# A Fourier mixing layer in front of a GELU MLP: the complex filter product summed on VectorE, narrower tiles in two stages of the transform

## The chip, the cores and the metric

The kernel runs on one core of a Trainium2 chip. The metric is the device time of one execution in microseconds; lower is better. The figure for the kernel before is the median of three runs; one more execution was taken with the hardware profiler, and all rows and timelines are from that one.

## The reference

Two layers in a row, on x of shape (8, 3008, 256). The first multiplies the spectrum of each batch along the sequence with a complex filter; the second is an MLP with the exact GELU.

```python
X = np.fft.rfft(x, axis=1)                       # 8 batches, 3008 points, 256 channels
y = np.fft.irfft(X * (filt_r + 1j * filt_i), n=3008, axis=1)
h = y.reshape(24064, 256) @ w_in                 # 256 -> 2048
out = (0.5 * h * (1 + erf(h / sqrt(2)))) @ w_out # 2048 -> 256
```

## The kernel before

**The transform.** 3008 = 47 x 64 (NA x NB). The transform is done in matmuls in two steps forward and two back. `s1` is the first forward step (over 47 points, four quarters c of each batch), `s2` the second (over 64 points, for 24 values of an index k), `s2_out` the product with the filter, `s3` the first step back (over 64), `s4` the last (over 47). Between `s1` and `s2`, and between `s3` and `s4`, the data go through DRAM (tensors R1 and R2), where the store and the load regroup them: `r1` loads the spectrum tiles `b_sb`, `r2` the tiles `d_sb`. Batch 0 has functions of its own (`c1`, `c1t`, `c2`, `c3`, `c3t`, `c4`) and runs before everything else, some 38 us. It uses the filters `F` as they were loaded; for batches 1 to 7 these are saved to DRAM (`save_filters`, tensor Fd) and loaded again in another order (`load_filters_again`).

**The MLP.** 24064 rows in 47 tiles of 512. `mm1` does the first matrix (line 635) and ScalarE the GELU (line 638). The second matrix is done for each tile but the first with seven products of quarter matrices in place of eight (`mm2_seven`, line 707). This needs sums of quarters of g on VectorE: `sums_1` (line 676), `sums_2` (line 682), `sums_3` (line 689). Its results are combined on VectorE as groups of output matmuls finish (lines 722 to 736): line 722 copies the first group, 724 and 727 add the third, 729 to 733 the fifth, 736 the last two. Two PSUM banks (`ps_o`) take turns: groups 1, 2 to 3, 4 to 5, 6 to 7. A bank is free for its next groups once VectorE has read it. Output rows are stored from GpSimd's queue (line 754).

**The order.** Tile code with a schedule written out by hand: 16 slots for each tile of the MLP, one `mm1` step (two 512-column matmuls and a GELU) and seven output matmuls to a slot. The transform of batch b is put into the slots of the tiles before its own, with `put(slot, function, ...)`, lines 902 to 978. Every engine runs its own instructions in that order, so an instruction that waits holds all behind it on its engine.

**A third of a batch.** Batches 1 to 7 do `s2`, `s2_out` and `s3` in three thirds u = 0, 1, 2; 21 thirds in all. `s2` of a third stands in slot s2[u], the four products in slots s2[u], +2, +4, +6, `s3` and the first half of its evacuation in slot +10 (+9 in two thirds of batch 1), the other half in the next slot. In a third, before:

- `s2` (line 458): 16 matmuls with stationary tiles of 64x64 and 256 moving columns, into four PSUM banks. The 64 stationary columns are real and imaginary part of 32 frequencies, so the two parts come to lie in different partitions.
- `s2_out` (line 470): four VectorE products of 128x1024, each of a bank (read twice over) with the real and the imaginary filter. The two halves of a complex product are left unsummed.
- `s3` (line 484): 16 matmuls of 64x64 and 512 columns. The summing of real and imaginary parts happens inside the contraction over 64 rows with the table `U`, accumulated over two values of t.
- `s3_out`: ScalarE evacuates four banks to `v_sb` (line 329), SP's queue stores them to R2.

PSUM has eight banks: three for `ps_h` (tag "h", also lent to one bank of each stage), two for `ps_o`, and three of tag "f" for the stages of the transform. The tables are built on GpSimd while the first slots run (`table_1_tiles`, `table_2_parities`, `table_u_rows`, `table_u_pick`, `table_4_rows`). The fold (lines 106 and 107) prepares x of the next batch on VectorE; its loads are issued from GpSimd's queue, each behind a `gate` (line 149), a one-element copy that waits for a product.

Of the kernel before, what the change touches and what calls it, by code (L numbers as in the profile page):

```python
# [31 lines left out]
class _Mix:  # L32
    def __init__(self, ctx, tc, x, filt_r, filt_i, w_in, w_out, out):
# [11 lines left out]
        self.pb = pool("pb", 3)  # L45
# [14 lines left out]
        self.U = c.tile([128, 2, 2, HB], BF16, name="U")  # L60
        self.T4a = c.tile([96, HB, 96], BF16, name="T4a")
        self.T4c = c.tile([96, NA, 2], BF16, name="T4c")
        self.F = c.tile([128, 2, K1, 256], BF16, name="F")
        self.w_in_sb = c.tile([128, 2, self.DFF], BF16, name="w_in_sb")
# [53 lines left out]
    def save_filters(self, k0, k):  # L118

        if "Fd" not in self.st:  # L120
            self.st["Fd"] = self.dram.tile([2, 2, 16, 2, K1, 256], BF16, tag="Fd", name="Fd")
        for t in range(2):
            for q in range(2):
                o = self.st["Fd"][:, q, :, t, k0:k0 + k, :].rearrange("a i k c -> i a (k c)")
                if q:
                    o = o[:, ::-1]
                self.nc.sync.dma_start(out=o, in_=self.F[32 * q:32 * q + 32, t, k0:k0 + k, :])

    def load_filters_again(self, eng, k0, k):

        for o in range(0, 128, 32):
            i = self.st["Fd"][o // 64, :, :, :, k0:k0 + k, :].rearrange("q i t k c -> (q i) t k c")
            f = self.F[o:o + 32, :, k0:k0 + k, :]
            if o < 64:
                eng.dma_start(out=f.rearrange("p t k c -> p t (k c)"), in_=i.rearrange("p t k c -> p t (k c)"))
            else:
                for t in range(2):
                    for e in range(2):
                        eng.dma_start(out=f[:, t, e::2], in_=i[:, t, 1 - e::2])
# [11 lines left out]
    def load_next(self, b, p, c, h):  # L151

        self.gate(self.st[b, "p", p][0:1, 0, 0:1])
        self.load_x_pairs(b + 1, c, h)
# [95 lines left out]
    def weights_4(self, g):  # L250


        ts = self.nc.gpsimd.tensor_scalar
        h, q, self.wt, self.wts = (g.tile([128, 1], FP32, name=n) for n in ("h48", "q48", "wt", "wts"))
        ts(out=h, in0=self.p, scalar1=48.0, scalar2=None, op0=ALU.is_ge)
        ts(out=q, in0=h, scalar1=-48.0, scalar2=-1.5, op0=ALU.mult, op1=ALU.add)
        self.nc.gpsimd.tensor_tensor(out=q, in0=self.p, in1=q, op=ALU.add)
        self.nc.gpsimd.tensor_tensor(out=q, in0=q, in1=q, op=ALU.mult)
        ts(out=q, in0=q, scalar1=2.25, scalar2=-1.0, op0=ALU.is_equal, op1=ALU.mult)
        ts(out=self.wt, in0=q, scalar1=2.0, scalar2=None, op0=ALU.add)  # L260
        ts(out=h, in0=h, scalar1=-2.0, scalar2=1.0, op0=ALU.mult, op1=ALU.add)
        self.nc.gpsimd.tensor_tensor(out=self.wts, in0=self.wt, in1=h, op=ALU.mult)
# [73 lines left out]
    def table_1_tiles(self, g):  # L336
# [4 lines left out]
        for r in (0, 64):  # L341
            v.tensor_copy(out=self.T1s[r:r + NA, 0:48], in_=self.T1[0:NA, 0:48])
# [10 lines left out]
    def table_u_rows(self, g):  # L353

        v = self.nc.gpsimd
        self.u0 = g.tile([128, 2, 2, HB], BF16, name="u0")
        v.tensor_copy(out=self.u0[:, 0], in_=self.T3[:, 0, :, 0:HB])
        v.tensor_copy(out=self.u0[:, 1], in_=self.T3i[:, 0, :, 0:HB])

    def table_u_pick(self, g):  # L360
        to = self.cols
        self.nc.gpsimd.iota(to, pattern=[[0, 2], [64, 2], [33, 2], [2, 16]], base=0, channel_multiplier=0,
                            allow_small_or_imprecise_dtypes=True)
        self.pick = g.tile([128, 128], BF16, name="pick")
        self.nc.gpsimd.tensor_scalar(out=self.pick, in0=to, scalar1=self.p, scalar2=None, op0=ALU.is_equal)

    def table_u(self):
        ps = self.bank("ps_u", "f")
        self.nc.tensor.matmul(ps[:, 0:128], lhsT=self.pick, rhs=self.u0.rearrange("p t r w -> p (t r w)"),
                              start=True, stop=True)  # L370
        self._evac(self.U.rearrange("p t r w -> p (t r w)"), ps[:, 0:128], "act")

    def table_4_rows(self, g):
# [3 lines left out]
        self.T1g = g.tile([NA, 2, 2, 12, 2, 2], BF16, name="T1g")  # L377
        self.T2g = g.tile([128, 2, 12, 2, 2], BF16, name="T2g")
        for x in range(2):
            for r in range(2):  # L380
                t = self.T1[0:NA, 24 * (x ^ r):24 * (x ^ r) + 24].rearrange("p (a k) -> p a k", k=2)
                for j in range(2):
                    v.tensor_copy(out=self.T1g[:, x, r, :, j], in_=t[:, :, ::-1] if j else t)
        t = self.T2.rearrange("p (a k) r j -> p r a j k", k=2)[:, 0, :, 0:2, :]
        for r in range(2):
            for j in range(2):
                v.tensor_copy(out=self.T2g[:, r, :, j], in_=t[:, :, j, ::-1] if j else t[:, :, j])

    def table_4_factors(self, g):
        ps = self.bank("ps_t4", "f")  # L390
        mm = lambda o, n, t, k: self.nc.tensor.matmul(ps[0:96, o:o + n], lhsT=t, rhs=self.eye[0:k, 0:k], start=True, stop=True)
        for x in range(2):
            mm(NA * x, NA, self.T1g[:, x].rearrange("p r a j k -> p (r a j k)"), NA)
        mm(128, 128, self.T2g.rearrange("p r a j k -> p (r a j k)"), 128)
# [46 lines left out]
    def r1(self, b, c):  # L441
        bt = self.pb.tile([128, 6, 256], BF16, tag="b", name="b_sb")
        self.st[b, "b", c] = bt
        v = self.st[b, "R1"].rearrange("n (r k) c -> (n r) k c", r=2)
        self.nc.sync.dma_start(out=bt, in_=v[:, 6 * c:6 * c + 6, :])


    def s2(self, b, u):

        nc = self.nc  # L450
        self.st[b, "ps2"] = ps = [[self.bank("ps_s2", "h" if i == d == 0 else "f") for d in range(2)] for i in range(2)]
        for i in range(2):
            for j in range(2):
                for odd in range(2):
                    for d in range(2):
                        k, r = 8 * u + 4 * i + 2 * j + odd, slice(64 * d, 64 * d + 64)
                        o = 64 * (odd ^ d)
                        nc.tensor.matmul(ps[i][d][o:o + 64, 256 * j:256 * j + 256],  # L458
                                         lhsT=self.T2p[r, k].rearrange("p a b c -> p (a b c)"),
                                         rhs=self.st[b, "b", k // 6][r, k % 6, :], start=True, stop=True)  # L460

    def s2_out(self, b, u, i, d):

        if d == 0:
            w = self.st[b, "w"] = self.pp.tile([128, 2, 4, 256], BF16, tag="p12", name="p12")
            for q in range(2):
                self.st[b, "p", 4 * u + 2 * i + q] = w[:, :, 2 * q:2 * q + 2].rearrange("p t a c -> p t (a c)")
        k = 8 * u + 4 * i + d
        ps = self.st[b, "ps2"][i][d].rearrange("p (a c) -> p a c", a=2)
        self.nc.vector.tensor_tensor(out=self.st[b, "w"][:, :, d:4:2, :], in0=ps.unsqueeze(1).to_broadcast([128, 2, 2, 256]),  # L470
                                     in1=self.F[:, :, k:k + 3:2, :], op=ALU.mult)

    def s3(self, b, u):

        nc = self.nc
        if u == 0:
            self.st[b, "R2"] = self.dram.tile([NB, 12, 4, 256], BF16, tag="R2", name="R2")
        ps = [[self.bank("ps_s3", "h" if i == par == 0 else "f") for par in range(2)] for i in range(2)]
        for i in range(2):
            for t in range(2):  # L480
                for q in range(2):
                    for par in range(2):
                        r = slice(64 * par, 64 * par + 64)
                        nc.tensor.matmul(ps[i][par][64 * q:64 * q + 64, :],  # L484
                                         lhsT=self.U[r, t].rearrange("p r w -> p (r w)"),
                                         rhs=self.st[b, "p", 4 * u + 2 * i + q][r, t, :], start=t == 0, stop=t == 1)
# [3 lines left out]
    def s3_out(self, b, u, i):  # L490
        ps = self.st[b, "ps3"][i]
        vt = self.pv.tile([128, 4, 256], BF16, tag="v", name="v_sb")
        for par in range(2):
            self._evac(vt[:, 2 * par:2 * par + 2, :].rearrange("p a b -> p (a b)"), ps[par],
                       False if b == u == i == par == 1 else "act")
        for q in range(2):
            self.nc.sync.dma_start(out=self.st[b, "R2"][:, 4 * u + 2 * i + q], in_=vt[64 * q:64 * q + 64])

    def r2(self, b, c):
        d = self.pd.tile([96, 8, 256], BF16, tag="d", name="d_sb")  # L500
        self.st[b, "d", c] = d
        R2 = self.st[b, "R2"].rearrange("(r w) a m c -> r (a m) w c", r=2)
# [36 lines left out]
    def c1t(self, q, eng):  # L539

        b = self.st[0, "b", q] = self.pb.tile([128, 6, 256], BF16, tag="b", name="b_sb")
# [5 lines left out]
        for i, e in enumerate(eng):  # L547
            self._evac(b[:, 0:4, :].rearrange("p a b -> p (a b)")[:, n * i:n * i + n], ps[:, n * i:n * i + n], e)
# [227 lines left out]
def kernel(  # L776
# [134 lines left out]
    for b in range(1, B):  # L911
# [5 lines left out]
        for c in range(4):  # L917
# [3 lines left out]
            put(r1 if c < 3 else s2[0] + 1, m.r1, b, c)  # L921
        for u in range(3):
            put(s2[u], m.s2, b, u)
# [8 lines left out]
        if b + 1 < B:  # L932
            for i, (u, o, p) in enumerate(((0, 5, 2), (0, 7, 2), (1, 1, 4), (1, 5, 6), (1, 7, 6), (2, 1, 8), (2, 5, 10), (2, 7, 10))):
# [35 lines left out]
    put(1, m.load_filters_again, nc.gpsimd, 0, 8)  # L969
    put(18, m.load_filters_again, nc.sync, 8, 16)  # L970
# [54 lines left out]
```

## Time and profile before

| What | us |
|---|---|
| three runs, median | 742.44 |
| lowest, highest | 742.04, 742.57 |
| the profiled execution | 742.11 |
| its span, from first to last instruction | 740.3 |

A group row reads: line, engine, operation, what it writes and reads, shapes, count, then busy us and mean ns of one, then the idle time of its engine just before such instructions and what ended it. A timeline row reads: start, duration, engine, line, operation, shapes, count; in brackets the idle time before it and what ended that. PE is TensorE, PEld its weight loads, DVE VectorE, ACT ScalarE, POOL GpSimd, SP SyncE. The granted TensorE clock is full in all slices. These two rows give VectorE's and ScalarE's largest groups outside the transform:

```profile
L638 ACT ACTIVATE g_sb<-ps_h 128x512 f16<-128x512 f32 x752 | 446.7, 602 | 145.3 <-PE ps_h L635 125.8
L676 DVE TENSOR_TENSOR s_sb<-g_sb 128x1024 f16<-128x1024 f16 x184 | 120.6, 689 | 1.0 <-ACT g_sb L638 1.0
```

### The profile page before, as it was taken

How to read it: one execution, taken by the hardware profiler on the slowest of the kernel's cores; microseconds unless marked ns; L12 is line 12 of the kernel's file. 1: busy time of each engine (PE TensorE's matmuls, PEld its weight loads, DVE VectorE, ACT ScalarE, POOL GpSimd, SP SyncE). 2: the span in 40 equal slices, each digit the busy share in tenths (PEclk: the TensorE clock that was granted, in tenths of full speed). 3: DMA queues.
4: the chain of work that ended last, by engine and by line, in shares of the span. 5: the costliest groups of instructions: out<-in, count | busy, mean ns of one | idle time of the engine just before them, and what ended most of it. 6: DMA issues, size and time to landing. Idle time of an engine off the chain costs nothing.

```text
span 740.3 us, 20857 instructions
## 1 busy us (share of the span) xinstructions
PE 722.4 (98%) x8448; PEld 507.2 (69%) x8588; DVE 584.6 (79%) x1036; ACT 574.7 (78%) x1048; POOL 293.4 (40%) x547
## 2 busy tenths in 40 slices
PE   8999999999999999999999999999999999999997
PEld 4856675666776666666677666666677766777776
DVE  7986988888878797788976889778888887675566
ACT  6997778678887888777887777877888787777773
POOL 7896446684313453134611364115531121122121
PEclk9999999999999999999999999999999999999999
DMA  8999643646255542645525456255544443311011
GB/s 146 220 204 238 161 111 97 198 101 136 75 154 150 132 104 93 176 117 126 124 94 157 127 118 144 72 158 138 110 103 136 137 118 99 93 38 51 31 58 58
DMA packets 83955, 90.79 MB, mean 123 GB/s; under 512 B 13347, under 2 KB 62883, under 8 KB 83731
## 3 DMA queue, kind: packets, MB, share of 16 engines
q1 hardware_dynamic: 60867, 48.98, 24.3%
q0 software_dynamic: 22576, 40.28, 23.7%
q8 instruction: 67, 1.10, 0.6%
q14 instruction: 29, 0.24, 0.1%
q10 hardware_dynamic: 416, 0.20, 0.1%
HBM read 57.15 MB, written 48.23 MB: 142 GB/s over the span
## 4 chain that ended last, share of the span: by engine, by line
PE 86%; ACT 6%; DVE 3%; issue 2%; DMA 2%; POOL 1%; DVEq 0%; POOLq 0%
PE ps_o L707 38%; PE ps_h L635 36%; ACT g_sb L638 3%; PE ps_s L484 3%; PE ps_s L513 3%; PE ps_s L429 2%; PE ps_s L458 2%; ACT y_sb L329 1%; ACT v_sb L329 1%; PE ps_o L648 1%; DMA x_sb<-in_x_dram 1%; DMA F<-in_filt_i_dram 1%; DVE g_sb L682 1%; PE ps_c L582 1%; DVE s_sb L676 1%
## 5 line engine op out<-in xcount | busy, mean ns | idle before, releaser
L638 ACT ACTIVATE g_sb<-ps_h 128x512 f16<-128x512 f32 x752 | 446.7, 602 | 145.3 <-PE ps_h L635 125.8
L635 PE MATMUL ps_h<-y_sb,w_in_sb 128*128 128x512 bf16 (+3 forms) x1464 | 416.2, 365 | 0.8 <-DVE a_sb L331 0.2
L754 POOL DMA_DIRECT2D out_dram<-ost x228 | 129.5, 574 | 390.1 <-DVE ost L736 368.3
L707 PEld LDWEIGHTS <-g_sb 128*128 128x128 f16 x2944 | 193.9, 98 | 83.6 <-issue 11.6
L707 PEld LDWEIGHTS <-s_sb 128*128 128x128 f16 x2208 | 147.9, 98 | 62.0 <-issue 11.1
L635 PEld LDWEIGHTS <-w_in_sb 128*128 128x128 bf16 x1600 | 125.0, 98 | 7.2 <-issue 1.1
L707 PE MATMUL ps_o<-w_sums,g_sb 128*128 128x128 f16 x1472 | 127.5, 219 | 1.8 <-DVE g_sb L682 0.9
L707 PE MATMUL ps_o<-w_sums,s_sb 128*128 128x128 f16 x1472 | 126.2, 219 | 1.7
L676 DVE TENSOR_TENSOR s_sb<-g_sb 128x1024 f16<-128x1024 f16 x184 | 120.6, 689 | 1.0 <-ACT g_sb L638 1.0
L707 PE MATMUL ps_o<-w_out_sb,g_sb 128*128 128x128 f16 x1472 | 118.9, 219 | 1.8
L470 DVE TENSOR_TENSOR p<-ps_s,F 128x1024 bf16<-128x1024 f32 x84 | 102.1, 1219 | 5.3 <-PE ps_s L458 4.0
L98 POOL DMA_DIRECT2D x_sb<-in_x_dram x156 | 79.1, 514 | 1.1 <-PE ps_c L611 0.7
L729 DVE TENSOR_TENSOR t_sb<-t_sb,ps_o 128x256 f32<-128x256 f32 x46 | 19.3, 420 | 59.5 <-PE ps_o L707 59.5
L682 DVE TENSOR_TENSOR g_sb<-s_sb,g_sb 128x1024 f16<-128x1024 f16 x92 | 65.0, 708 | 1.6
L707 PE MATMUL ps_o<-w_out_sb,s_sb 128*128 128x128 f16 x736 | 63.9, 219 | 0.3
L689 DVE TENSOR_TENSOR s_sb<-g_sb 128x1024 f16<-128x1024 f16 x92 | 64.1, 697 | 0.0
L736 DVE TENSOR_TENSOR ost<-t_sb,ps_o 128x256 f32<-128x256 f32 x90 | 33.7, 416 | 20.1 <-PE ps_o L707 20.1
L329 ACT ACTIVATE y_sb<-ps_s 128x376 bf16<-128x376 f32 x94 | 46.7, 497 | 3.2 <-PE ps_s L513 3.2
L513 PEld LDWEIGHTS <-d_sb 96*128 96x128 bf16 x448 | 31.3, 97 | 25.3
L329 ACT ACTIVATE v_sb<-ps_s 128x512 bf16<-128x512 f32 x83 | 45.0, 596 | 0.5 <-ACT g_sb L638 0.3
L331 DVE CAST a_sb<-ps_s 128x512 bf16<-128x512 f32 x54 | 34.7, 684 | 12.7 <-PE ps_s L429 12.4
L724 DVE TENSOR_TENSOR ost<-t_sb,ps_o 128x256 f32<-128x256 f32 x46 | 19.1, 416 | 25.9 <-PE ps_o L707 25.9
(155 smaller groups left out, 526.4 us busy)
## 6 DMA issues: line engine op xcount, KB each, us to landing
out_dram<-ost POOLq DMA_DIRECT2D x126, 128.0 KB, 2.4
b_sb<-R SPq DMA_DIRECT2D x28, 384.0 KB, 3.9
R<-v_sb SPq DMA_DIRECT2D x84, 128.0 KB, 2.7
d_sb<-R SPq DMA_DIRECT2D x56, 192.0 KB, 3.6
R<-a_sb SPq DMA_DIRECT2D x108, 96.0 KB, 2.2
x_sb<-in_x_dram POOLq DMA_DIRECT2D x48, 94.0 KB, 2.7
x_sb<-in_x_dram POOLq DMA_DIRECT2D x48, 48.0 KB, 2.8
x_sb<-in_x_dram POOLq DMA_DIRECT2D x12, 188.0 KB, 5.2
```

The source lines that it names most:

```text
L98: self.nc.gpsimd.dma_start(out=xt[64 * v + to:64 * v + to + m, h, 4 * c:4 * c + 4 * n, :], in_=xv[h][at:at + m, w:w + 4 * n, :])
L329: self.nc.scalar.activation(out=out, in_=in_, func=AF.Copy, scale=1.0 if scale is None else scale)
L331: self.nc.vector.tensor_copy(out=out, in_=in_)
L470: self.nc.vector.tensor_tensor(out=self.st[b, "w"][:, :, d:4:2, :], in0=ps.unsqueeze(1).to_broadcast([128, 2, 2, 256]), in1=self.F[:, :, k ...
L513: nc.tensor.matmul(ps[:, 94 * i:94 * i + 94], lhsT=d[:, (grp % 2) * 4 + i, 128 * half:128 * half + 128], rhs=self.T4a[:, 4 * grp + i, 0:2 ...
L635: nc.tensor.matmul(ps[:, o:o + n], lhsT=w[:, dc], rhs=self.ring[:, dc, off:off + n], start=(dc == 0), stop=(dc == 1))
L638: nc.scalar.activation(out=self.st["g", t][:, jc, :], in_=ps, func=AF.Gelu)
L676: self.nc.vector.tensor_tensor(out=self.st["s", t][:, i:i + 2], in0=a, in1=b, op=ALU.subtract)
L682: self.nc.vector.tensor_tensor(out=a21[:, k], in0=self.st["s", t][:, k, 0], in1=a22[:, k], op=ALU.add)
L689: self.nc.vector.tensor_tensor(out=self.st["s4", t][:, k], in0=a12[:, k], in1=s2[:, k], op=ALU.subtract)
L707: nc.tensor.matmul(ps[:, (m + 1) % 2, sub, :], lhsT=a[:, i, 128 * sub:128 * sub + 128], rhs=b[:, i], start=i == 0, stop=i == 7)
L754: eng.dma_start(out=out, in_=tile_[lo - r0:lo - r0 + n])
```

## The change

For batches 1 to 7 the real and imaginary part of a frequency now lie side by side in the free dimension of one partition, and the complex product is completed on VectorE before the step back.

- `s2`: 32 matmuls of 64x32 and 256 columns in place of 16 of 64x64. The order over k changes: a third u holds k = 6c + 2u + m for c = 0 to 3 and m = 0, 1. The four c lie in four groups of 32 partitions.
- `s2_out`: the same four products of 128x1024, in another layout. After the second product of each m, two more instructions of 128x512 in bf16: a subtraction (real part) and an addition (imaginary part).
- `s3`: 32 matmuls of 32x64 and 256 columns in place of 16 of 64x64 and 512, over the summed halves only.
- `r1`: three loads of a third each in place of four of a quarter; the third one is issued behind the first forward third. Two tiles `b_sb` (pool `pb`) in place of three, each larger; batch 0 puts two of its parts into one tile.
- Filters: saved in 16 DMAs in place of 8, loaded again in 8 in place of 20, with half the bytes; they take up half of `F`.
- Tables: `U` smaller, and the columns of `T1s`, `T1g`, `T2g` and the weights of the last step follow the new order of k. The slots stay as they are.

```diff
     def load_filters_again(self, eng, m0, m):
+        for t in range(2):
+            for a in range(2):
+                i = self.st["Fd"][a, t, :, :, :, m0:m0 + m, :].rearrange("c q i m d -> (c q i) (m d)")
+                eng.dma_start(out=self.Fu[:, t, a, m0:m0 + m, :].rearrange("p m d -> p (m d)"), in_=i)
...
-    def r1(self, b, c):
-        bt = self.pb.tile([128, 6, 256], BF16, tag="b", name="b_sb")
+    def r1(self, b, u):
+        bt = self.st[b, "b", u] = self.pb.tile([128, 8, 256], BF16, tag="b", name="b_sb")
...
     def s2(self, b, u):
+        for m in range(2):
+            for r in range(2):
+                for c in range(4):
                     for d in range(2):
-                        nc.tensor.matmul(ps[i][d][o:o + 64, 256 * j:256 * j + 256],
-                                         lhsT=self.T2p[r, k].rearrange("p a b c -> p (a b c)"),
-                                         rhs=self.st[b, "b", k // 6][r, k % 6, :], start=True, stop=True)
+                        p = slice(64 * d, 64 * d + 64)
+                        nc.tensor.matmul(ps[m][d][32 * c:32 * c + 32, 256 * r:256 * r + 256],
+                                         lhsT=self.T2p[p, 6 * c + 2 * u + m, r].rearrange("p a b -> p (a b)"),
+                                         rhs=self.st[b, "b", u][p, 2 * c + m, :], start=True, stop=True)
...
     def s2_out(self, b, u, m, d):
+        w, a, v = self.st[b, "p", 2 * u + m], m ^ d, self.nc.vector.tensor_tensor
+        ps = self.st[b, "ps2"][m][d].rearrange("p (r c) -> p r c", r=2)
+        f = self.Fu[:, :, a, 2 * u + m, :]
+        v(out=w[:, a], in0=ps.unsqueeze(2).to_broadcast([128, 2, 2, 256]),
+          in1=f.unsqueeze(1).to_broadcast([128, 2, 2, 256]), op=ALU.mult)
+        if d:
+            v(out=w[:, :, 0, 0], in0=w[:, :, 0, 0], in1=w[:, :, 1, 1], op=ALU.subtract)
+            v(out=w[:, :, 0, 1], in0=w[:, :, 0, 1], in1=w[:, :, 1, 0], op=ALU.add)
...
     def s3(self, b, u):
+        ps = [self.bank("ps_s3", "f" if c else "h") for c in range(4)]
+        for m in range(2):
             for t in range(2):
-                for q in range(2):
-                    for par in range(2):
+                for c in range(4):
+                    for a in range(2):
+                        p = slice(32 * c, 32 * c + 32)
+                        nc.tensor.matmul(ps[c][64 * a:64 * a + 64, 256 * m:256 * m + 256], lhsT=self.U[p, t],
+                                         rhs=self.st[b, "p", 2 * u + m][p, a, 0, t, :], start=t == 0, stop=t == 1)
...
     def table_1_tiles(self, g):
-        for r in (0, 64):
-            v.tensor_copy(out=self.T1s[r:r + NA, 0:48], in_=self.T1[0:NA, 0:48])
+        for p in (0, 64):
+            for r in (0, K1):
+                v.tensor_copy(out=self.T1s[p:p + NA, r:r + K1].rearrange("p (u c m) -> p u c m", c=4, m=2),
+                              in_=self.T1[0:NA, r:r + K1].rearrange("p (c u m) -> p u c m", u=3, m=2))
...
-            put(r1 if c < 3 else s2[0] + 1, m.r1, b, c)
         for u in range(3):
+            put(r1 if u < 2 else s2[0] + 1, m.r1, b, u)
```

## The prediction

> **What bounds the kernel now.** I read the page's busy shares and chain first, then the groups by shape, then the timeline of TensorE and VectorE around one third of a batch (batch 4, u = 0), since a share says nothing about where a wait ends.
>
> ```profile
> PE 722.4 (98%) x8448; PEld 507.2 (69%) x8588; DVE 584.6 (79%) x1036; ACT 574.7 (78%) x1048; POOL 293.4 (40%) x547
> ...
> PE 86%; ACT 6%; DVE 3%; issue 2%; DMA 2%; POOL 1%; DVEq 0%; POOLq 0%
> ```
>
> TensorE sets the end: 98% busy and 86% of the chain. In the timeline its instructions follow each other at their streaming pace (0.216 us for each 512-column matmul, 0.056 for each 128-column one), so a microsecond taken off it is gained, and one in which it waits is lost.
>
> ```profile
> L484 PE MATMUL ps_s<-p,U 64*64 64x512 bf16 x336 | 22.2, 382 | 0.7
> L458 PE MATMUL ps_s<-b_sb,T2p 64*64 64x256 bf16 x336 | 13.4, 275 | 1.0
> L470 DVE TENSOR_TENSOR p<-ps_s,F 128x1024 bf16<-128x1024 f32 x84 | 102.1, 1219 | 5.3 <-PE ps_s L458 4.0
> L736 DVE TENSOR_TENSOR ost<-t_sb,ps_o 128x256 f32<-128x256 f32 x90 | 33.7, 416 | 20.1 <-PE ps_o L707 20.1
> ```
>
> The first two rows are the matmuls of the two changed stages, the third the filter products. They run in 21 thirds (batches 1 to 7, u = 0 to 2) of 16, 16 and 4 instructions. TensorE, in order of time:
>
> ```profile
> 320.20 0.63 PE L458 MATMUL ps_s<-b_sb,T2p 64*64 64x256 bf16 x16
> 320.77 0.56 PE L707 MATMUL ps_o<-w_out_sb,g_sb 128*128 128x128 f16 x7
> ...
> 329.10 1.06 PE L484 MATMUL ps_s<-p,U 64*64 64x512 bf16 x16
> 330.09 0.56 PE L707 MATMUL ps_o<-w_sums,s_sb 128*128 128x128 f16 x7
> ```
>
> From its first matmul to the next line's, a forward third takes 0.56 us (320.20 to 320.77), an inverse third 0.99 (329.10 to 330.09). Four matmuls overlap: sixteen of 256 columns in 0.56 us are four rounds of 0.109 plus about 0.1 to drain, sixteen of 512 are four of about 0.22 plus the same. VectorE at the same place:
>
> ```profile
> 323.80 1.22 DVE L470 TENSOR_TENSOR p<-ps_s,F 128x1024 bf16<-128x1024 f32 x1
> 324.94 0.41 DVE L722 COPY t_sb<-ps_o 128x256 f32<-128x256 f32 x1
> 325.27 1.22 DVE L470 TENSOR_TENSOR p<-ps_s,F 128x1024 bf16<-128x1024 f32 x1
> 326.40 0.68 DVE L689 TENSOR_TENSOR s_sb<-g_sb 128x1024 f16<-128x1024 f16 x1
> 327.00 1.22 DVE L470 TENSOR_TENSOR p<-ps_s,F 128x1024 bf16<-128x1024 f32 x1
> 328.13 0.41 DVE L724 TENSOR_TENSOR ost<-t_sb,ps_o 128x256 f32<-128x256 f32 x1
> 328.58 0.42 DVE L727 TENSOR_TENSOR t_sb<-t_sb,ps_o 128x256 f32<-128x256 f32 x1
> 328.92 0.69 DVE L689 TENSOR_TENSOR s_sb<-g_sb 128x1024 f16<-128x1024 f16 x1
> 331.29 0.42 DVE L729 TENSOR_TENSOR t_sb<-t_sb,ps_o 128x256 f32<-128x256 f32 x1 [1.69 <-PE ps_o L707]
> ```
>
> This is what decides. VectorE is 79% busy on average, but from the first product (320.73) to 329.6 it has no gap; its idle time (1.69 us) comes after the inverse stage has begun. The last product ends at 328.22, the inverse stage starts at 329.10: 0.88 us of slack.
>
> **The change, part by part.** *Forward matmuls.* 32 of 64x32 instead of 16 of 64x64, still 256 columns. With eight at once that is again four rounds of 0.109: no gain, no loss. *Inverse matmuls.* 32 of 32x64 and 256 columns instead of 16 of 64x64 and 512: four rounds of 0.109 instead of 0.216, so 4 x 0.107 = 0.43 us less, 21 x 0.43 = 9.0 us. The trace has no 32-row or 32-column tile. The bound on the good side is 9.0; on the bad side stands the fastest sustained rate of the trace, four starts per 0.109 us: 32 would take eight rounds, 0.97 plus some 0.06 for pauses = 1.03 us, so +0.47 forward and +0.04 inverse, 21 x 0.51 = 10.7 us lost. I take 9.0: two by two tiles overlap fully, and eight weight loads of 47x64 start and end within 0.14 us (first stage, 210 us).
>
> On this rate the Trainium skill ("TensorE: Matmul & The Clock Gate", section "Wait — 56ns, not 53.3ns?") speaks against the change: start to start of two matmuls never falls below about 25 ns. By it 32 would take an estimated 0.8 us, and the sum would be some 10 us worse. The 16 weight loads of a forward third lie in 0.36 us here, 22 ns each, last one's duration included, so I don't read it as a floor across tiles.
>
> *Sums on VectorE.* Two more instructions per (u, m), 512 bf16 elements each: 84. Nearest rows: 256 elements at one per cycle take 0.416 us (L736), 1024 16-bit elements at two per cycle 0.689 (L676). 512 at two per cycle is as many cycles as the first: 0.42. Ends: a 512-element 16-bit scalar operation 0.34 (L316), 512 elements out of PSUM in float 0.68 (L569). An instruction that doesn't need the one before starts 0.09 before its end (323.80 to 324.94 is 1.14 for 1.22), one that needs it 0.04 after (L729 to L730, 0.46 for 0.42). The first sum needs the product before it: 0.13 more for the product, then 2 x 0.33: 0.78 us per pair, 1.57 per third.
>
> *Where that lands.* The pair of m = 0 stands before L722, that of m = 1 before L724 and L727. (a) L722 frees the bank for the third group of output matmuls; its slack is 0.70 in the regular thirds, so 0.78 + 0.06 (smallest hand-over seen) - 0.70 = 0.14 late. This lies inside what follows. (b) The inverse stage's last round, due 0.35 us after its first matmul, needs the last sum: it is late by 1.57 + 0.06 - 0.35 = 1.28 less the third's slack. The slacks read off the timeline, batch by batch: -0.05, -0.31, 0.80; 0.37, 0.89, 0.88; 0.89, 0.88, 1.22; 0.88, 0.88, 1.22; 0.40, 1.22, 0.89; 0.88, 1.22, 0.88; 1.15, 2.10, 2.17. The waits come to 3.4 + 1.7 + 0.85 + 0.86 + 1.33 + 0.86 + 0.13 = 9.1 us. Behind the waiting matmul stand the slot's other matmuls, then the gelu and the evacuations L329 on ScalarE; these have 0.27 us idle after the first pair (331.12), about what they are later by. (c) In u = 2 of batches 2 to 6 the fold (L106, L107) stands between the products and L727, and the fifth output group has only 0.76, 1.10, 1.10, 0.77, 0.76 us of slack. L727 is 1.57 + 0.06 late less that: 0.87, 0.53, 0.53, 0.86, 0.87, where wait less gain left these thirds at -0.03, -0.37, -0.37, -0.04, -0.03: 4.5 us more in all. After each third VectorE's idle gap takes up the rest.
>
> *At nothing.* Saving the filters: 16 DMAs for 8, at 0.83 us on SP's queue 6.6 us more, while that queue is idle from 25.6 to 43.0; uncovered it would hold the first stage's stores. Reload: 4 issues for 10 on each of GpSimd's and SP's queues and half the bytes, in a stretch (40 to 65 us) whose DMA share is 0.98; TensorE is idle 0.6 us of it, so at most that is won. Spectrum loads: three for four, the same bytes, the third behind the first forward third as before, 20 us ahead of its use. Tables on GpSimd: two T1s copies more (0.25 each) and one copy less before the x loads, one comparison more (1.13) before T2p: the fold that uses the x loads starts behind VectorE's own work (38.73), T2p is first used at 64.6; uncovered, 0.5 us. The batch-0 tiles now come in pairs, but their waits are on matmuls already past. The gate of the next x loads waits 0.78 longer, tens of us ahead of need.
>
> Sum: -9.0 + 9.1 + 4.5 = **+4.6 us**, against the profiled execution's own 742.1 (span 740.3 and 1.8 around it) 746.7; the median is 0.3 higher, so 747.0. With sums of 0.34 (1.24 per third) the waits are 4.1, (c) 4.0: -0.9, 741.5. With 0.68 (2.6 per third) the waits are 29, (c) 4.5: +24.5, 767. Waits put on the whole tile instead of the half cost up to 0.1 per third, 2 more.
>
> **The rivals.** *The gain stands.* If the sums hide, TensorE keeps 21 x 0.43 = 9.0, or 21 x 0.27 = 5.7 where ScalarE's evacuations bind behind the inverse stage: 733.4 to 736.7. For it: VectorE's 2.5 us idle per third (1.69 and 0.84). Against: none of it lies between products and inverse stage. It decides where a third's sums delay VectorE by under some 0.8 us, half of the 1.57: (b) is then 1.6, (c) 2.0, the sum -5.4. *Eight tiles don't overlap* (the change does not do what it says): TensorE loses 10.7; the forward third's 0.47 gives VectorE that much slack, so of the waits some 3 us stay: 756. It decides as soon as a third's 32 starts take over 0.75 us. For it: double the instructions and no such tile in the trace. *Sums at one element per cycle*: 767, from 0.55 us each on. Against: L682 reads runs of 256 at two per cycle (0.708).
>
> **How the numbers follow.** The forecast (sums on the path, 0.34 to 0.5 us each) has 0.62, its own range 741.5 to 752; the gain stands 0.20, no overlap 0.13, slow sums 0.05. This kernel's measurements tell about 0.2%, 1.5 us, from no change. Within the forecast 0.03 falls below 740.9 and 0.12 within 1.5 us. So faster 0.23, same 0.12, slower 0.65. 736 to 757 leaves out half of the first rival and the slow tails.
>
> **What would show it.** Right: inverse thirds that stream in 0.56 us but with a pause before their second half, waiting for VectorE; sums near 0.42; VectorE's 1.69 us gap nearly gone; batch 1 loses most, batch 7 gains. Wrong: inverse thirds of 0.56 without a pause, or a forward third near 1 us.

## The result and the profile after

The changed kernel takes 750.39 us, the median of five runs (749.98 to 751.74), against 742.44 (742.04 to 743.11) before: a ratio of 1.0108, interval 1.0093 to 1.0123, or 8.0 us more. 747.0 was predicted, with slower at 0.65.

The busy shares and the chain of the changed kernel:

```profile
PE 730.8 (98%) x9261; PEld 508.9 (68%) x9261; DVE 616.9 (82%) x1120; ACT 575.1 (77%) x1048; POOL 288.2 (39%) x544
...
PE 77%; DVE 15%; DMA 3%; POOL 2%; issue 2%; ACT 0%; DVEq 0%; POOLq 0%; SPq 0%
```

VectorE's busy time rose by 32.3 us (584.6 to 616.9), and its share of the chain from 3% to 15%: TensorE still sets the end, but it now waits for VectorE on the way. TensorE's busy times can't be compared: the trace of before lacks some matmul records (8448 matmuls beside 8588 weight loads, here 9261 of each), so its 722.4 us are too few. The rows of the two changed stages, which are whole, fell from 35.6 to 32.4 us (13.4 and 22.2, now 13.5 and 18.9).

Groups by shape, changed kernel. L485 is the step back (484 before), L471 and L472 are the two sums; in the timelines below L457 is the second forward step (458), L468 the product (470), and 724, 726, 729 and 738 are the lines 722, 724, 727 and 736 of before:

```profile
L485 PE MATMUL ps_s<-p,U 32*64 32x256 bf16 x672 | 18.9, 282 | 1.1 <-DVE p L468 0.6
L472 DVE TENSOR_TENSOR p<-p 128x512 bf16<-128x512 bf16 x42 | 18.3, 436 | 0.0
L471 DVE TENSOR_TENSOR p<-p 128x512 bf16<-128x512 bf16 x42 | 18.1, 432 | 1.4
```

84 new VectorE instructions cost 36.4 us of its time, 0.43 each. The same third as before the prediction (batch 4, u = 0), TensorE and then VectorE in order of time:

```profile
326.51 0.63 PE L457 MATMUL ps_s<-b_sb,T2p 64*32 64x256 bf16 x32
327.08 0.56 PE L709 MATMUL ps_o<-w_out_sb,g_sb 128*128 128x128 f16 x7
...
335.57 0.93 PE L485 MATMUL ps_s<-p,U 32*64 32x256 bf16 x32
336.43 0.56 PE L709 MATMUL ps_o<-w_sums,s_sb 128*128 128x128 f16 x7
```

```profile
331.38 0.43 DVE L471 TENSOR_TENSOR p<-p 128x512 bf16<-128x512 bf16 x1
...
332.06 0.42 DVE L724 COPY t_sb<-ps_o 128x256 f32<-128x256 f32 x1
...
334.12 1.22 DVE L468 TENSOR_TENSOR p<-ps_s,F 128x1024 bf16<-128x1024 f32 x1
335.37 0.42 DVE L471 TENSOR_TENSOR p<-p 128x512 bf16<-128x512 bf16 x1
335.72 0.42 DVE L472 TENSOR_TENSOR p<-p 128x512 bf16<-128x512 bf16 x1
```

The forward third is as long as before, 0.57 us (326.51 to 327.08). The inverse third takes 0.86 (335.57 to 336.43) where it took 0.99. Its rounds of eight begin at 0, 0.13, 0.28 and 0.61 us: the last waits for the sum that ends at 336.14. In the last two thirds of batch 7 nothing is missing; there the rounds begin at 0, 0.13, 0.24 and 0.35 and the third is over in 0.57.

**Where the 8 us come from.** Both kernels have the same 5152 output matmuls, so the start of each can be compared with its start in the trace of before. This offset is -0.28 us at the first (the traces differ by themselves in the start-up), and +8.06 at the last, 8.34 more. By stretches:

| Stretch | predicted, us | measured, us |
|---|---|---|
| batch 1, up to the first third of batch 2 | +2.1 | +3.19 |
| batch 2, u = 0 | +0.5 | +1.82 |
| the 14 other thirds of batches 2 to 6, without the next row | -1.3 | -0.86 |
| fifth output group behind L729, five times | +4.5 | +4.38 |
| batch 7 | -1.2 | -0.19 |
| sum | +4.6 | +8.34 |

What TensorE waited for (waits, changed kernel: the wait, us in all, how often, the longest):

```profile
PE ps_o L709 <- DVE t_sb L729: 3.5, 5, 0.7
PE ps_o L709 <- DVE ost L738: 2.1, 3, 0.7
PE ps_s L512 <- DVE p L468: 1.7, 1, 1.7
```

The first line is the predicted wait of the u = 2 thirds. The second is the bank of a tile's second output group; one of the three, in batch 1, takes the place of lateness that was predicted for that third, the other two were not predicted, nor was the third line. For it, the timeline of all engines at batch 2, u = 0:

```profile
148.09 1.62 POOL L411 TENSOR_TENSOR tmp_sb<-t_sb 96x376 f32<-96x376 f32 x2
149.28 0.72 DVE L471 TENSOR_TENSOR p<-p 128x512 bf16<-128x512 bf16 x1
...
149.92 1.20 DVE L472 TENSOR_TENSOR p<-p 128x512 bf16<-128x512 bf16 x1
...
151.04 1.30 DVE L691 TENSOR_TENSOR s_sb<-g_sb 128x1024 f16<-128x1024 f16 x1
152.27 1.21 DVE L468 TENSOR_TENSOR p<-ps_s,F 128x1024 bf16<-128x1024 f32 x1
...
153.63 0.33 PE L512 MATMUL ps_s<-T4a,d_sb 96*128 96x94 bf16 x4 [1.69 <-DVE p L468]
```

GpSimd builds a piece of the last step's table (L411) at just this time. Beside it the sums take 0.72 and 1.20 instead of 0.42, and L691 1.30 instead of 0.68. The third product, which must read its PSUM bank before an `s4` matmul (L512) may have it, comes late, and TensorE stands for 1.69 us.

### The profile page after: what moved, and what is told of

Read it like the earlier page. It is cut to its first block, busy times and chain, and to the rows that moved or that the text cites. A ratio compares the mean times of both kernels' runs of the same rounds, so it can differ in the third digit from the quotient of the medians.

```text
span 748.6 us, 22400 instructions
## 1 busy us (share of the span) xinstructions
PE 730.8 (98%) x9261; PEld 508.9 (68%) x9261; DVE 616.9 (82%) x1120; ACT 575.1 (77%) x1048; POOL 288.2 (39%) x544
## 4 chain that ended last, share of the span: by engine, by line
PE 77%; DVE 15%; DMA 3%; POOL 2%; issue 2%; ACT 0%; DVEq 0%; POOLq 0%; SPq 0%
PE ps_h L637 35%; PE ps_o L709 33%; DVE p L468 5%; DMA x_sb<-in_x_dram 3%; PE ps_s L512 2%; PE ps_s L430 2%; DVE s_sb L678 2%; POOL out_dram L756 1%; PE ps_s L485 1%; DVE p L472 1%; PE ps_s L457 1%; DVE g_sb L684 1%; PE ps_o L650 1%; DVE s_sb L691 1%; DVE x_sb L108 1%
## 5 line engine op out<-in xcount | busy, mean ns | idle before, releaser
L637 PE MATMUL ps_h<-y_sb,w_in_sb 128*128 128x512 bf16 (+3 forms) x1600 | 445.3, 366 | 0.2 <-DVE a_sb L328 0.2
L709 PEld LDWEIGHTS <-g_sb 128*128 128x128 f16 x2944 | 193.9, 98 | 90.1 <-issue 13.5
L678 DVE TENSOR_TENSOR s_sb<-g_sb 128x1024 f16<-128x1024 f16 x184 | 120.3, 687 | 0.8 <-ACT g_sb L640 0.8
L468 DVE TENSOR_TENSOR p<-ps_s,F 128x1024 bf16<-128x1024 f32 x84 | 102.1, 1217 | 3.5 <-PE ps_s L457 1.8
L691 DVE TENSOR_TENSOR s_sb<-g_sb 128x1024 f16<-128x1024 f16 x92 | 63.8, 693 | 0.0
L731 DVE TENSOR_TENSOR t_sb<-t_sb,ps_o 128x256 f32<-128x256 f32 x46 | 19.3, 419 | 40.9 <-PE ps_o L709 39.7
L512 PEld LDWEIGHTS <-d_sb 96*128 96x128 bf16 x448 | 31.2, 97 | 27.2 <-issue 2.2
L738 DVE TENSOR_TENSOR ost<-t_sb,ps_o 128x256 f32<-128x256 f32 x90 | 33.7, 415 | 18.1 <-PE ps_o L709 18.1
L726 DVE TENSOR_TENSOR ost<-t_sb,ps_o 128x256 f32<-128x256 f32 x46 | 19.1, 416 | 24.7 <-PE ps_o L709 24.1
```

The costliest lines, as they stand in the source:

```text
L468: v(out=w[:, a], in0=ps.unsqueeze(2).to_broadcast([128, 2, 2, 256]), in1=f.unsqueeze(1).to_broadcast([128, 2, 2, 256]), op=ALU.mult)
L512: nc.tensor.matmul(ps[:, 94 * i:94 * i + 94], lhsT=d[:, (grp % 2) * 4 + i, 128 * half:128 * half + 128], rhs=self.T4a[:, 4 * grp + i, 0:2 ...
L637: nc.tensor.matmul(ps[:, o:o + n], lhsT=w[:, dc], rhs=self.ring[:, dc, off:off + n], start=(dc == 0), stop=(dc == 1))
L678: self.nc.vector.tensor_tensor(out=self.st["s", t][:, i:i + 2], in0=a, in1=b, op=ALU.subtract)
L691: self.nc.vector.tensor_tensor(out=self.st["s4", t][:, k], in0=a12[:, k], in1=s2[:, k], op=ALU.subtract)
L709: nc.tensor.matmul(ps[:, (m + 1) % 2, sub, :], lhsT=a[:, i, 128 * sub:128 * sub + 128], rhs=b[:, i], start=i == 0, stop=i == 7)
```

## The experiments

Theory: the narrow tiles give 0.41 us in each inverse third; all of it and 8 us more goes into sums that stand on VectorE ahead of what TensorE needs next. Rivals: the tiles or the loads cost time themselves; ScalarE's evacuations bind; the sums cost by their number and not by their place.

In the table are the medians less the median of before on the same chip, and the offset of the last output matmul less that of the first, from the profiled run. The second is free of the start-up, which puts the first output matmul anywhere between 63.2 and 65.0 us in these traces.

| Kernel | median, us | less before, us | by the trace, us | ratio to before, with interval |
|---|---|---|---|---|
| changed kernel | 750.39 | +7.95 | +8.34 | 1.0108 (1.0093 to 1.0123) |
| e1, no sums | 734.51 | -7.84 | -8.27 | 0.9892 (0.9878 to 0.9907) |
| e2, half the sums | 740.60 | -1.75 | -1.98 | 0.9977 (0.9967 to 0.9988) |
| e3, table earlier | 749.55 | +7.20 | +6.85 | 1.0093 (1.0078 to 1.0108) |
| e4, sums and step back later | 741.89 | -0.46 | -0.83 | 0.9988 (0.9978 to 0.9997) |
| e5, all thirds later | 742.47 | -0.12 | -1.37 | 0.9998 (0.9988 to 1.0007) |
| e6, only the step back later | 753.61 | +11.02 | +11.30 | 1.0151 (1.0136 to 1.0166) |
| e7, only the sums later | 762.20 | +19.61 | +19.38 | 1.0265 (1.0246 to 1.0284) |
| e8, e4 and one copy on ScalarE | 739.84 | -2.44 | -3.04 | 0.9967 (0.9955 to 0.9979) |
| e9, before with that copy alone | 743.37 | +1.09 | +1.00 | 1.0013 (1.0005 to 1.0022) |
| e10, e8 and later folds | 739.87 | -2.41 | -3.06 | 0.9969 (0.9957 to 0.9981) |

**Without the sums.** The matmuls stay as changed; the complex product is left incomplete.

```diff
-        if d:
-            v(out=w[:, :, 0, 0], in0=w[:, :, 0, 0], in1=w[:, :, 1, 1], op=ALU.subtract)
-            v(out=w[:, :, 0, 1], in0=w[:, :, 0, 1], in1=w[:, :, 1, 0], op=ALU.add)
```

> The changed kernel without the two sums on VectorE (the inverse stage reads the unsummed real-filter products, so the output is not the reference's). Theory (the narrow tiles save 9.0 us on TensorE, and all of the loss is waits behind the sums): 21 x 0.43 = 9.0 us under the kernel before, 733 us, or up to 736.7 if ScalarE's evacuations bind; inverse thirds of 0.56 us without a pause. Rival (the narrow tiles or the other parts of the change cost time themselves): 742 us or more.

The batch 4, u = 0 third of this kernel (L482 is the step back, L706 the output matmul):

```profile
326.06 0.64 PE L482 MATMUL ps_s<-p,U 32*64 32x256 bf16 x32
326.63 0.56 PE L706 MATMUL ps_o<-w_sums,s_sb 128*128 128x128 f16 x7
```

734.51 us: the theory's range. The inverse third takes 0.57, and from batch 1's third third on each third gains 0.41 to 0.42 in the trace, nowhere less. The two thirds before that, whose slack in the kernel before was negative (-0.05 and -0.31), gain 0.31 and 0.05. So the narrow tiles overlap as reckoned, no ScalarE limit appears behind them (0.27 was the prediction's guess of what would remain), and the loads and tables cost nothing visible behind the first output matmul. Ahead of it the traces scatter by up to 1.8 us, and a smaller cost would not be seen. The sums cost 7.95 + 7.84 = 15.8 us.

**With half of them.** Only the addition is left out.

```diff
-            v(out=w[:, :, 0, 1], in0=w[:, :, 0, 1], in1=w[:, :, 1, 0], op=ALU.add)
```

> The changed kernel without the addition (the imaginary part stays unsummed, so the output is not the reference's); 42 sums instead of 84. Theory (each third loses only what the sums exceed its slack by, so the loss is not in proportion): the delay of VectorE is 0.9 us a third instead of 1.6; worked with the slacks of the kernel before, waits of some 2.5 in the inverse stage and 4 at the banks against 9.0 gained: about 740 us, under the kernel before. Rival (VectorE's busy time as a whole is what costs, in proportion): half way between 733 and 750.4, about 742.

Half of the sums costs 740.60 - 734.51 = 6.1 us, the other half 9.7. In the thirds u = 0 and 1 of batches 3 to 6 half of them costs nothing: the trace has each at the full gain of 0.41. There a delay costs nothing until it has used up the slack (0.88 us, and the 0.35 after which the last round is due), so it is a matter of a threshold, not a price per instruction. In u = 2 thirds half of them still delay the fifth output group, by 0.3 to 0.7.

**The table earlier.** One of four pieces of GpSimd's work, moved by 8 slots.

```diff
-    for i, slot in enumerate((15, 80, 96, 112)):
+    for i, slot in enumerate((15, 80, 96, 104)):
```

> The changed kernel with the last part of the GpSimd table (slot 112, in which the first third of batch 2 starts) moved to slot 104. Theory (GpSimd's work stretches the 16-bit sums from 0.42 to 0.72 and 1.2 us there, which holds a last-stage matmul for 1.7 us): the pause of 1.7 us goes, 749 us against 750.4; the sums of that third take 0.42 each. Rival (the pause comes from the sums' number alone): 750.4, no change.

The timeline of this kernel, same place as the last fence above:

```profile
150.24 0.42 DVE L472 TENSOR_TENSOR p<-p 128x512 bf16<-128x512 bf16 x1
...
152.54 0.33 PE L512 MATMUL ps_s<-T4a,d_sb 96*128 96x94 bf16 x4
```

Both sums are back at 0.42 (the second is shown, which took 1.20), and batch 2, u = 0 costs 0.29 us by the trace instead of 1.82. This settles the mechanism. For the time it is less plain: the trace has 1.5 us less, the medians 0.75, and the two intervals overlap.

**Sums and step back later, together and singly.** In batches 2 to 6 the sums move behind L726 and L729 (seventh slot after the third's start), the step back from slot 10 to 12, behind them. For this the two sums get a function of their own, `s2_sum`; of the edit only the slots are shown.

```diff
+            if 1 < b < B - 1:
+                for i in range(2):
+                    put(s2[u] + 7 + (b == 2 and u == 0), m.s2_sum, b, u, i)
-            s3 = s2[u] + (9 if b == 1 and u != 1 else 10)
+            s3 = s2[u] + (9 if b == 1 and u != 1 else 12 if 1 < b < B - 1 else 10)
```

> The changed kernel with, in batches 2 to 6, the four sums of a third put behind the fourth product and the output sums L726 and L729 (slot +7), and the inverse stage two slots later (+12). The same instructions, in another order. Theory (what costs is that the sums stand in front of products, bank releases and the inverse stage): in these 15 thirds the loss of 5.3 us becomes a gain of 4.0 (0.27 each) to 6.4 (0.43 each): 739 to 741.5 us. Rival (VectorE has too much work as a whole): within 2 us of 750.4.

The timeline of this kernel (L476 and L477 are the sums, L731 and L734 were L726 and L729, L490 is the step back):

```profile
329.82 0.41 DVE L731 TENSOR_TENSOR ost<-t_sb,ps_o 128x256 f32<-128x256 f32 x1
330.26 0.42 DVE L734 TENSOR_TENSOR t_sb<-t_sb,ps_o 128x256 f32<-128x256 f32 x1
330.60 0.42 DVE L476 TENSOR_TENSOR p<-p 128x512 bf16<-128x512 bf16 x1
...
331.61 0.42 DVE L477 TENSOR_TENSOR p<-p 128x512 bf16<-128x512 bf16 x1
...
332.58 0.64 PE L490 MATMUL ps_s<-p,U 32*64 32x256 bf16 x32
```

The same sums, the same 0.42 each, and 7.95 + 0.46 = 8.4 us less than in the changed kernel. They now fill what was VectorE's idle time ahead of the fifth group's first sum (L736 here, L729 in the kernel before, where it was 1.69 us); the products are followed at once by the instructions that free the output banks, and the step back (332.58) finds the sums done (332.03). The u = 0 and 1 thirds of batches 3 to 6 have the full 0.41. The median lies just above the 739 to 741.5 us expected: in the u = 2 thirds, which have a fold on VectorE as well, the step back still takes 0.73 to 0.83 us. Each half of the move alone:

```diff
-            s3 = s2[u] + (9 if b == 1 and u != 1 else 10)
+            s3 = s2[u] + (9 if b == 1 and u != 1 else 12 if 1 < b < B - 1 else 10)
```

> The changed kernel with the inverse stage of batches 2 to 6 two slots later (+12), the sums left where they are. Theory (a sum in front of L729 holds the bank of the fifth output group; the inverse stage in front of that group was what covered it): the pause in the inverse stage goes, but the fifth group now comes 0.99 us sooner and waits in every third, 0.5 in the ordinary ones and 1.5 to 1.9 in the last of a batch: some 9 us lost in these 15 thirds instead of 5.3, 754 us. Rival (only the inverse stage's own wait matters): the 0.3 to 0.4 each of the ordinary thirds come back, 745 to 747.

```diff
+            if 1 < b < B - 1:
+                for i in range(2):
+                    put(s2[u] + 7 + (b == 2 and u == 0), m.s2_sum, b, u, i)
```

> The changed kernel with the sums of batches 2 to 6 behind the output sums (slot +7), the inverse stage left at +10. Theory: no bank waits any more, but the last sum ends 0.97 us after its round is due in an ordinary third, and 2 us in one with a fold: +0.55 and +1.5 to +1.9 net, some 14 us in these 15 thirds: 759 us. Rival (bank waits are the main loss): they go, 746 or less.

Both are slower than the changed kernel: 753.61 and 762.20. With only the step back moved, its thirds take 0.57, yet an ordinary third costs 0.10 more than before: its 0.41 are gained and 0.51 lost again at the output banks, since L726 and L729 still stand behind the sums, and the fifth output group waits even in u = 0 thirds. With only the sums moved, the banks come in time, but the step back stands ahead of sums that are not done: its weight loads wait, and from its first matmul on it takes 1.25 us (waits of that kernel; 759 us were expected):

```profile
PEld L490 <- DVE p L476: 17.2, 15, 2.1
```

So there are two deadlines behind the products, the output bank and the step back. The changed kernel misses both by a little; moving one thing makes one of them worse. The sums' price lies in their place.

**The rest of the loss.** First batch 1 and batch 7 in the same manner, with batch 1's thirds three, two and one slots earlier, its four products evenly spaced, the folds of batches 3 to 7 three slots later, and the table moved as above:

```diff
-        s2 = (33, 45, 57) if b == 1 else ...
+        s2 = (30, 43, 56) if b == 1 else ...
...
-            s3 = s2[u] + (9 if b == 1 and u != 1 else 10)
+            s3 = s2[u] + (10 if b == 1 else 12 if b < B - 1 else 11 if u == 0 else 10)
```

> The order of the run before (sums behind the output sums, inverse stage later) carried to all thirds: batch 1 starts its thirds three, two and one slots earlier, with its sums at +7 and the inverse stage at +10; the first third of batch 7 has its sums at +8; the fold starts three slots later, and the table part of slot 112 is at 104. Theory: what is left of the loss in the reordered run (3.2 us in batch 1, some 0.6 in the last third of batches 2 to 6, 0.9 in batch 7) goes, and 21 x 0.41 = 8.7 us are gained: 734 to 737 us. Rival (the order only moves the waits, VectorE has no room for the sums in batch 1): 741 or more.

This missed: 742.47 where 734 to 737 was expected, no better than e4 by the medians. By the trace batch 1 costs 2.95 us instead of 3.21. The first third now costs 0.10 instead of 0.97, but the next two tiles' second output groups wait longer or as long behind L743, which was 738 (1.16 and 0.90 us by the offsets, 0.75 and 0.90 in e4), and the other two thirds cost 0.85 instead of 0.60. Batch 7's first third still costs 0.50 (0.65 in the changed kernel). Batch 1's slots lie between the filters' reload and the due slot of its own rows, and no order tried here fits its sums in.

Second, less VectorE work per tile: the copy of the first output group (L724) goes to ScalarE, on top of e4 and the table's move. The same copy in the kernel before shows what it is worth alone.

```diff
-                nc.vector.tensor_copy(out=t1, in_=p1)
+                nc.scalar.copy(out=t1, in_=p1)
```

> The reordered run (sums of batches 2 to 6 at +7, inverse stage at +12) with the table part of slot 112 at 104, and the copy L724 of the first output group moved from VectorE to ScalarE in all 46 tiles. Theory (what is left of the loss, 3.2 us in batch 1, some 0.6 in the last third of batches 2 to 6, 0.9 in batch 7, is VectorE being late by fractions of a microsecond, so each 0.33 us taken from it in front of a wait is gained there): 739 us. Rival (the copies hold up the gelu on ScalarE, or the rest has another cause): 741.5 or more.

> The kernel before with only that copy on ScalarE. Theory (TensorE waits for VectorE nowhere in it, so taking work off VectorE buys nothing): 742.4, within 1 us. Rival (the move is a gain by itself, whatever the filter product does): 740 or less.

739.84 us: 2.4 us under the kernel before and, each against its own runs of before, 10.4 under the changed one. Of the kernels that do the whole computation only this one and e10 below are clearly faster than the one before; e4's interval ends at 0.9997. VectorE's time fell by 19.5 us (616.9 to 597.4), ScalarE's rose by 9.8, and ScalarE, at 79%, had the room. In the kernel before the copy alone loses 1.09 us, all of it at one place, as its trace shows:

```profile
81.31 0.37 ACT L722 COPY t_sb<-ps_o 128x256 f32<-128x256 f32 x1
81.73 0.44 PE L707 MATMUL ps_o<-w_out_sb,g_sb 128*128 128x128 f16 x5 [0.84 <-ACT t_sb L722]
```

There the copy stands behind two gelus and an output group waits 0.84 us for it. So the copy is no gain by itself; it gives room that only the added sums need.

Last, the folds of batches 3 to 7 two slots later on top of e8:

```diff
-            put(... else s1 - 28 + e + 6 * c, m.fold, b, c)
+            put(... else s1 - 26 + e + 6 * c, m.fold, b, c)
```

> The run with the copy on ScalarE, and the folds of batches 3 to 7 two slots later, so that the first one no longer stands in front of the output sums and the sums of the last third. Theory: the pauses of some 0.25 us each in the inverse stage and in front of the fifth output group of those thirds go, 737.5 to 738.5 us. Rival (the fold then holds L738 and the bank behind it instead): no gain over the run without it.

No gain, as the rival said: 739.87. Its trace has the three remaining pauses of 0.17 us gone (u = 2 of batches 2, 5 and 6), but TensorE then loses some 0.2 before the next batch's third in their stead, and the offsets end alike (-3.04 and -3.06).

## Why the prediction was right, and where it fell short

The range put on record, 736 to 757 us, lies on both sides of no change, so that the number fell into it says little. What can be tested is the mechanism and its terms.

**Bound and decision point: right.** TensorE's end moved by what VectorE did between the products and the next deadline. The average idle time of VectorE, 21% before, was no help to it; e4 shows that it helps only when the sums stand inside it.

**Matmuls: right.** The forward third stayed at 0.57, the inverse third gives 0.41 (predicted 0.43) where nothing is late: 21 x 0.41 = 8.6. The rival of eight tiles that don't overlap is out. The rule of the Trainium skill that was weighed ("TensorE: Matmul & The Clock Gate", section "Wait — 56ns, not 53.3ns?"), 25 ns at the least from start to start, gives an estimated 0.8 us for 32 matmuls, and the trace has 0.57. As a floor across tiles of the array it does not hold here.

**Sums: right.** 0.42 in the regular thirds, 1.57 us per third; both rivals of other speeds are out.

**The waits, (a) and (b): right in their sum.** An ordinary third was predicted at -0.04 and came to +0.03. The late L724 (a) shows as a wait of its own, 0.17 at the third output group, and the inverse third then pauses 0.29 (0.86 less 0.57): together 0.46, where 0.40 was predicted with (a) inside (b). One third (batch 5, u = 0) was predicted at +0.45 from a slack of 0.40 read off the trace, and behaves like the others, +0.03. That slack was not the third's own. In the trace of before VectorE waited ahead of it for a store of output rows:

```profile
407.33 0.42 DVE L730 TENSOR_TENSOR ost<-t_sb,ps_o 128x256 f32<-128x256 f32 x1 [1.18 <-DMA out_dram<-ost]
```

So the first product came 1.02 us behind the third's first matmul, against 0.53 in batch 4. The trace of e9, which has the same order but for one copy, shows this wait too (1.05 us); the changed kernel's has none, and its product comes after 0.55.

**The bank behind L729, (c): right.** 4.38 of 4.5 predicted, five times 0.87.

**"After each third VectorE's idle gap takes up the rest": wrong at two places.** After the last third of batch 1 and the first of batch 7 no idle gap follows in time. The last sums stand, with one sum of quarters (L678) between, ahead of the tile's final L738, which frees the bank for the next tile's second output group. The timeline of the changed kernel in batch 7, VectorE and TensorE:

```profile
600.15 0.42 DVE L472 TENSOR_TENSOR p<-p 128x512 bf16<-128x512 bf16 x1
...
601.09 0.74 DVE L738 TENSOR_TENSOR ost<-t_sb,ps_o 128x256 f32<-128x256 f32 x2
...
601.88 0.44 PE L709 MATMUL ps_o<-w_out_sb,g_sb 128*128 128x128 f16 x5 [0.73 <-DVE ost L738]
```

By the offsets that is 0.90 + 0.89 = 1.8 us. The prediction followed a deadline inside the tile and none across its end.

**The sums at a constant 0.42: wrong at one place.** In batch 2, u = 0, GpSimd's table work stretches them, and what waits is an `s4` matmul, which the prediction had not named: 1.82 us instead of 0.48, so 1.3 more. The trace of before had a hint: L689 took 1.09 us there instead of 0.69.

4.6 + 1.8 + 1.3 = 7.7 of 8.3. In the rest, 13 thirds cost 0.07 more each than reckoned, batch 5's first 0.4 less, and batch 1 some 0.2 more.

**At nothing: right** as far as e1 can show: with the sums out, saving, reloading, spectrum loads and tables leave the full gain in 19 thirds. Of the rivals "the gain stands" came nearest, but only with another place for the sums, and then with 0.5 (e4) to 2.4 us (e8) of the 5.7 to 9.0 that it named. Even there batch 1 keeps a loss of 2.6 to 3.2 us and batch 7 one wait of 0.9. A version that removes these was not found.

## What to carry to other kernels

Work moved from the bounding engine to one with idle time is worth what that engine can do between its input and the next thing somebody waits for, not what its average share leaves. For an added instruction, list every deadline behind it in its engine's order (the consumer of its result, each buffer that is freed behind it, the one across the end of the loop too), take the slack of each from the trace, and move the instruction and its consumer together if they miss. Then look at what the neighbouring engines do at that moment: a duration measured in a quiet stretch may not hold in a busy one.

## What the runs showed of the hardware

- Thirty-two matmuls on 64x32 or 32x64 tiles with 256 columns take 0.57 us from the first start to the next instruction: rounds of eight, 0.11 to 0.13 apart. That is 18 ns a matmul on average. Four row groups that write four PSUM banks at once cost nothing that can be seen.
- 16-bit VectorE instructions with both inputs in SBUF stretch beside elementwise work on GpSimd, 0.42 to 0.72 and 1.20 us, 0.68 to 1.30, while products with one input in PSUM stay at 1.21 in the same stretch. The Trainium skill says so in kind ("GPSIMD Engine Reference", section "1. Specifications": GpSimd's SBUF interfaces are shared with VectorE, and two SBUF inputs contend). The size, a factor of up to 2.9, is from this trace.
- The first output matmul starts between 63.2 and 65.0 us in these traces, although nearly the same work runs up to there. Differences under a microsecond were better read from offsets behind that point than from one run's time.
